# Two more output blocks of the last batch as Strassen products, their last stores in parts, and two of the first z turns copied by another engine

## The chip, the cores and the metric

The kernel runs on one core of a Trainium2 chip. The metric is the device time of one execution in microseconds (us); four executions are given for the kernel before. A core has a matrix engine, TensorE (PE in the profile, with its weight loads as PEld); a vector engine, VectorE (DVE); a scalar engine, ScalarE (ACT); GpSimd (POOL); and SyncE (SP), which here only issues DMAs. ACT and POOL issue DMAs too. Each engine runs its own instructions in order, and they wait for one another by semaphores. Matmuls write PSUM, which DVE and ACT read; everything else lies in the on-chip memory SBUF.

## The reference

Attention with squared positive scores, gated by `u`, then a feed-forward layer with a sigmoid gate. B is 8, S is 3008, D is 256, z has 64 columns, the hidden layer 2048.

```python
scores = scale * np.matmul(z, z.transpose(0, 2, 1))   # scale = 1 / S
attn = np.maximum(scores, 0.0) ** 2
x = (u * np.matmul(attn, v)).reshape(B * S, D)
h = x @ w_in
g = h * (1.0 / (1.0 + np.exp(-1.702 * h)))
out = g @ w_out
```

The scores are symmetric, since both sides are z.

## The kernel before

**Batches and blocks.** The eight batches follow one another. Within a batch the 3008 rows are cut into six column blocks of 512 (the last has 448; half a tile of 64 rows at the end of a batch is put together with that of its neighbour, so that an odd batch has a full last block and an even one a block of 384). Per batch the kernel runs attention for blocks 0 to 5, then the feed-forward layer for blocks 0 to 5. The order of every engine's instructions is that of the program text; nothing is reordered afterwards. PE's order is thus written out by hand: score matmuls (`take`, `scores`) are put between the steps of `attend` by the tables `SCHED`, `SCHED0`, `TAIL`, and so on.

**Attention.** `scores` multiplies z with z into a PSUM tile `sc`, two 512-wide halves at a time (from the tag `ps2`, two buffers). `square` lets ACT take the positive part (`rl`, L231) and DVE square it (`a`, L245). Where the mirrored block is wanted, SP issues a DMA that turns `a` into `tt` (L251). `attend` multiplies V with `a` or `tt` into `o` (L304), and DVE multiplies it with the turned `u` (L321).

**The start.** All engines are idle at first, and z of the first batch has to be turned before any scores can be made. Z comes in six pieces g of four tiles. `first_cast(g)` lets DVE write z in 16 bit twice side by side (L123); `first_zt(g)` lets PE transpose the four tiles into a PSUM tile `zp` (L129) and copies that to `ZT` with a rearrangement (L137): turn 0 by ACT, all others by DVE. Turns 0 and 1 stand before the loop. Turns 2 to 5 are put at steps n = 2, 7, 13 and 21 of the first `attend` (the table `FIRST_ZT`), and each is followed by the casts for the next turn. The pair of scores that needs turn 2 stands at step 6, that for turn 3 at step 14, that for turn 4 at step 22 (`SCHED0`). Meanwhile POOL casts V to 16 bit (L172), and SP issues the loads of z, V and the first u, and between them the turning DMAs.

**The feed-forward layer.** `up_group(b, q)` makes two of sixteen rows of hidden tiles for one block (four matmuls of 128x512, L345), ACT applies the gate (`gf`, L353) and DVE scales it to 16 bit (`gt`, L354). Eight groups make a block, 48 a batch; the first 20 are put between the steps of the last `attend`, and 28 are left.

The product with `w_out` is done in two ways. For blocks 0 to 3 (`k < NST`) it is one level of Strassen's scheme in Winograd's form: the block's row tiles are split by parity `o`, the hidden rows into halves and the output channels into halves `C0` and `C1`, and seven products P1 to P7 of half size take the place of eight. Each product (`product`, L441) is 16 matmuls of 128x128, each with its own weights. The left operands are sums S1 to S4 of parts of `gt`, made by DVE in two halves each (`left_sum`, L408 to L416); `up_group` takes one such sum from the list `SUMS` after its own work, so that they spread out. The products of a block share three PSUM tiles from the tag `ps1` (four buffers): P1, P6, P7 and P4 add onto one, P5 and P3 onto another, P2 has its own. After P1, P6 and P7 ACT copies the bank to a small SBUF tile (`uP1`, `uP6`, `uP7`, one buffer each, L451), before the next product adds on. The outputs are then: P2 + `uP1` (parity 0, `C0`), P5 + `uP7` after P7 (parity 1, `C1`), P5 with P3 + `uP6` after P3 (parity 0, `C1`), all by DVE (L457), and after P4 a copy by ACT (parity 1, `C0`, L453). `products` gives the order: each P1 of a block comes before P4 and P3 of the block before. After each of the 28 up groups stands one product, and 28 is also their number. After P3 of a block SP stores it.

Blocks 4 and 5 are done plainly. In batches 0 to 6 `down64` does it in 64-row pieces (L520), with the next batch's first scores in between. In the last batch `down` does it (L475): 16 matmuls of 128x256 per row tile, eight row tiles, with copies by ACT (L481) after every second one. `store` writes block 4 in one DMA, and the last block in three pieces of 128x2x256, 128x256 and twice 64x256, all issued by ACT (L493, L499).

**The queues around the change.** At the end SP's queue holds the stores of blocks 0 to 3, ACT's the copies and the stores of blocks 4 and 5, and POOL's nothing. At the start SP's queue holds the loads of z and V, then two turning DMAs, four loads of u (L187), and the rest of the turning DMAs.

Of the kernel before, what the change touches and what calls it, by code (L numbers as in the profile page):

```python
# [9 lines left out]
F32 = mybir.dt.float32  # L10
F16 = mybir.dt.float16
P = 128
# [3 lines left out]
def kernel(  # L16
# [13 lines left out]
    AF = mybir.ActivationFunctionType  # L30
# [9 lines left out]
    CH = 512  # L40
# [84 lines left out]
    def first_zt(g):  # L125
        z2 = ZT["st"][g // CB][:, g % CB * CB:(g % CB + 1) * CB]
        zp = ps1.tile([P, CB, P], F16, name="zp", tag="ps1")
        for k in range(CB):
            pe.transpose(zp[:, k, :], z2[:, k, :, :], ident)  # L129
        zt = ZT[0][:, g * CB:(g + 1) * CB, :].rearrange("d n p -> d (n p)")  # L130
        nb = CB if g < NCH - 1 else CB - 1
        dst = zt[:, :nb * P].rearrange("d (p n) -> d p n", n=nb)
        src = zp[:, :nb, :].rearrange("d n p -> d p n")
        if g == 0:
            act.activation(dst, src, AF.Copy, scale=1.0)
        else:
            dve.tensor_copy(dst, src)  # L137
        if nb < CB:
            dve.tensor_copy(zt[:, nb * P:], zp[:, nb, :])
# [194 lines left out]
    def blocks(b):  # L334

        return [(i, CH if i < NCH - 1 or b % 2 else LFULL) for i in range(NCH)]

    def up_group(b, q):
        k, fg = divmod(q, NFG)
        i, n = blocks(b)[k]  # L340
        hg = ps2.tile([P, FFG, CH], F32, name="hg", tag="ps2")
        for e in range(FFG):
            ff = fg * FFG + e
            for c in range(NCC):
                pe.matmul(  # L345
                    hg[:, e, :n], W1[:, c, ff * P:(ff + 1) * P], XT[b, i][:, c, :n],
                    start=(c == 0), stop=(c == NCC - 1),
                )
        if fg % 2 == 0:
            GT[b, k, fg // 2] = pa.tile([P, CB, CH], F16, name="gt", tag="tt", bufs=14)  # L350
        g = GT[b, k, fg // 2][:, (fg % 2) * FFG:(fg % 2 + 1) * FFG, :n]
        gf = pw.tile([P, FFG, CH], F32, name="gf", tag="gf")
        act.activation(gf[:, :, :n], hg[:, :, :n], AF.Gelu_apprx_sigmoid, scale=1.0 / FSC)  # L353
        dve.tensor_scalar(g, gf[:, :, :n], FSC, None, ALU.mult)  # L354
        if SUMS:
            SUMS.pop(0)()
        if k < NST and fg == NFG - 1:
            SUMS.extend(left_sums(b, k) + (weight_sums() if b == k == 0 else []))


# [3 lines left out]


    NST = 4
    SUMS, ST = [], {}
    LO, HI = slice(0, NFF // 2), slice(NFF // 2, NFF)
    C0, C1 = slice(0, P), slice(P, D)
# [45 lines left out]
        else:  # L415
            dve.tensor_tensor(s_, a12, ST[b, k, "S2", h], ALU.subtract)  # L416

    def products():

        lst = []  # L420
        for k in range(NST):
            one = [(k, "P6"), (k, "P5"), (k, "P7"), (k, "P2")]
            lst += [(k, "P1")] + ([(k - 1, "P4"), (k - 1, "P3")] if k else []) + one
        return lst + [(NST - 1, "P4"), (NST - 1, "P3")]

    def product(b, k, name):
        right = {
            "P1": W2[:, LO, C0], "P2": W2[:, HI, C0], "P3": W2[:, HI, C1], "P4": WT[:, 3],
            "P5": WT[:, 0], "P6": WT[:, 1], "P7": WT[:, 2],
        }[name]  # L430
        if name in ("P1", "P2", "P5"):
            ST[b, k, "bank" + name] = ps1.tile([P, 2, P], F32, name="st", tag="ps1")
        bank = ST[b, k, "bank" + {"P6": "P1", "P7": "P1", "P4": "P1", "P3": "P5"}.get(name, name)]
        for m in range(2):
            for ff in range(NFF // 2):
                h, f = divmod(ff, CB)
# [4 lines left out]
                pe.matmul(  # L441
                    bank[:, m, :], lhs()[:, f, m, :], right[:, ff, :],
                    start=name in ("P1", "P2", "P5") and m == 0 and ff == 0,
                    stop=ff == NFF // 2 - 1, skip_group_check=True,
                )
# [14 lines left out]
        if name == "P3":  # L460
            store(b, k, CB - 1, sp)

    def down_list(b):
        return [(k, s, h) for k, (i, n) in enumerate(blocks(b)) if k >= NST for s in range(n // P) for h in range(2)]

    def down(b, k, s, h):
        i, n = blocks(b)[k]
        ns = n // P
        if s == 0 and h == 0:
            Y[b, k] = pw.tile([P, CB, D], F32, name="y", tag="y")  # L470
        if s % 2 == 0 and h == 0:
            Y["ps"] = ps1.tile([P, 2, D], F32, name="yp", tag="ps1")
        yp = Y["ps"]
        for ff in range(h * NFF // 2, (h + 1) * NFF // 2):
            pe.matmul(  # L475
                yp[:, s % 2, :], GT[b, k, ff // CB][:, ff % CB, s * P:(s + 1) * P], W2[:, ff, :],
                start=(ff == 0), stop=(ff == NFF - 1),
            )
        if h == 1 and (s % 2 == 1 or s == ns - 1):
            s0 = s - s % 2  # L480
            act.activation(Y[b, k][:, s0:s + 1, :], yp[:, :s % 2 + 1, :], AF.Copy, scale=1.0 / FSC)  # L481
        if h == 1:
            store(b, k, s)

    def store(b, k, s, eng=act):
        i, n = blocks(b)[k]
        ns = n // P
        r0 = b * S + i * CH
        full = min(n, S - i * CH) // P
        final = b == B - 1 and k == NCH - 1  # L490
        if s == ns - 1 or final and s % 2 == 1:
            s0 = s - 1 if final else 0
            eng.dma_start(  # L493
                out[r0 + s0 * P:r0 + min(full, s + 1) * P].rearrange("(n p) c -> p n c", p=P),
                Y[b, k][:, s0:min(full, s + 1), :],
            )
        if s == ns - 1 and full < ns:
            for h_, bb in enumerate((b, b - 1)):
                (act if b == B - 1 else pool).dma_start(  # L499
                    out[bb * S + S0:(bb + 1) * S], Y[b, k][h_ * SREM:(h_ + 1) * SREM, full, :],  # L500
                )


    def down64(b, k):
# [8 lines left out]
        def step(n):  # L513
# [18 lines left out]
                        Y[b, k] = pw.tile([P, CB, D], F32, name="y", tag="y")  # L532
                    act.activation(Y[b, k][:, m * per:(m + 1) * per, :], yp[m][:, :per, :], AF.Copy, scale=1.0 / FSC)
            if n == len(order) - 1:
                store(b, k, ns - 1, pool)

        return turns, [lambda n=n: step(n) for n in range(len(order))]

# [51 lines left out]
    def take(b, n):  # L590
        for post_ in scores(b, [queue.pop(0) for _ in range(n)]):
            post_()
# [17 lines left out]
    posts[0]()  # L610
    first_cast(2)
    posts[1]()
    take(0, 1)
    load_u(0, 1)

    for b in range(B):
# [3 lines left out]
        for i in range(NCH):  # L620
            for n, step in enumerate(attend(b, i, b == 0 and i < 2)):
                if b == 0 and i == 0 and n == 5:
                    load_u(0, 0)
                if b == 0 and i == 0 and n in FIRST_ZT:
                    first_zt(FIRST_ZT[n])
                    if FIRST_ZT[n] + 1 < NCH:
                        first_cast(FIRST_ZT[n] + 1)
                if (i, n) in turn:
                    turn_u(b, turn[i, n])
# [10 lines left out]
        if more:  # L640
# [3 lines left out]
            for n0 in range(0, NJ, VB):  # L644
                load_v(b + 1, n0, sp)
            fill(b + 1)
        downs, prods = down_list(b), products()
        for q in range(head, nup):
            if more and q in (head + 14, head + 20):
                k = int(q == head + 20)  # L650
                turn_u(b + 1, k)
                load_u(b + 1, k + 2)
            up_group(b, q)
            product(b, *prods.pop(0))
        if more:
            while downs[0][0] < NCH - 2:
                down(b, *downs.pop(0))
            for k in range(NCH - 2, NCH):
                turns, steps = down64(b, k)
                at = {n: 3 - len(turns) for n in turns} | TAIL[len(turns)]  # L660
                for n, step in enumerate(steps):
                    take(b + 1, at.get(n, 0))
                    step()
        else:
            for d in downs:
                down(b, *d)


# [28 lines left out]
```

## Time and profile before

| what | us |
|---|---|
| four executions | 1207.62, 1209.11, 1210.41, 1211.33 |
| their median | 1209.76 |
| the profiled execution, by the same clock | 1211.33 |
| its span, first to last instruction | 1209.5 |

The profiled execution is one of the four. The granted TensorE clock was 0.999 over the span. The busy time of the engines by stretch, from the windows view:

```profile
0.00:10.00 10.00, 7.42 (x35) 2.68 (x35) 4.66 (x11) 5.49 (x6) 2.77 (x10) 1.00 0.76 240
10.00:20.00 10.00, 5.62 (x37) 2.30 (x36) 8.00 (x15) 4.14 (x5) 9.23 (x13) 1.00 1.15 264
20.00:30.00 10.00, 10.00 (x52) 3.33 (x50) 8.27 (x13) 7.69 (x8) 2.66 (x5) 1.00 1.22 175
...
1160.00:1170.00 10.00, 10.00 (x119) 7.45 (x118) 8.28 (x16) 7.13 (x10) 0.00 (x0) 1.00 0.01 3
...
1180.00:1190.00 10.00, 10.00 (x114) 7.17 (x112) 5.16 (x9) 6.43 (x9) 0.00 (x0) 1.00 0.17 54
1190.00:1200.00 10.00, 10.00 (x102) 9.04 (x100) 1.03 (x2) 2.22 (x3) 0.00 (x0) 1.00 0.22 73
1200.00:1210.00 10.00, 4.83 (x45) 4.08 (x42) 0.00 (x0) 1.19 (x2) 0.00 (x0) 1.00 0.27 86
```

Each row is a stretch from A to B in us after the start and its length, then the busy time and the number of instructions of PE, PEld, DVE, ACT and POOL, then the granted clock of PE, the mean busy share of the 16 DMA engines, and what they moved in GB/s. Between 10 and 20 us PE is busy 5.62 of 10 us; from 20 us on it is busy throughout, until after 1200 the matmuls end. In the rows quoted below, "x16" counts instructions of one kind that follow each other, and a time in brackets is idle time of that engine and who ended it.

### The profile page before, as it was taken

Reading aid. Unit: us, or ns where it says so; the run is one execution under the profiler, and the core shown is the slowest. Engines: PE = TensorE matmul, PEld = TensorE weight load, DVE = VectorE, ACT = ScalarE, POOL = GpSimd, SP = SyncE. Lnnn points to the kernel's source line nnn. Section 1 sums busy time; section 2 is a strip of 40 time slices with the busy share of each in tenths; the row PEclk is TensorE's granted clock in tenths of the full one; section 3 lists DMA queues with packets and bytes.
Section 4 is the critical chain, followed back from the end, with each engine's and each line's share of the span. In section 5 each row is a group of like instructions: output and inputs, shape, how many; then the busy total and the mean of one; then the engine's idle time right before and its main releaser. Section 6 shows DMA issues by size and latency. Waiting matters only on the chain.

```text
span 1209.5 us, 28025 instructions
## 1 busy us (share of the span) xinstructions
PE 1193.3 (99%) x11689; PEld 718.7 (59%) x11689; DVE 819.0 (68%) x1257; ACT 768.6 (64%) x897; POOL 306.4 (25%) x361
## 2 busy tenths in 40 slices
PE   7999999999999999999999999999999999999998
PEld 2446765467654685446765468554775547844576
DVE  6669954597546975469654696648966489564882
ACT  5777684476845767357683666736677376762763
POOL 4145300452004620044200451015510134101000
PEclk9999999999999999999999999999999999999999
DMA  9966389562994539854399443974449764596012
GB/s 228 164 110 126 117 167 156 89 150 74 182 158 85 140 93 173 147 85 136 93 188 140 81 137 97 192 131 77 139 122 188 126 88 146 115 175 112 1 37 70
DMA packets 366111, 152.32 MB, mean 126 GB/s; under 512 B 313248, under 2 KB 358048, under 8 KB 365984
## 3 DMA queue, kind: packets, MB, share of 16 engines
q1 hardware_dynamic: 328960, 113.16, 48.1%
q0 software_dynamic: 35392, 35.80, 14.6%
q8 instruction: 91, 1.49, 0.5%
q10 hardware_dynamic: 1632, 1.57, 0.4%
q14 instruction: 36, 0.29, 0.1%
HBM read 60.29 MB, written 24.64 MB: 70 GB/s over the span
## 4 chain that ended last, share of the span: by engine, by line
PE 96%; DMA 2%; DVE 1%; ACT 1%; issue 0%; SPq 0%; ACTq 0%
PE o L304 38%; PE hg L345 26%; PE st L441 17%; PE yp L520 8%; PE sc L217 6%; DMA tt<-a 1%; PE yp L475 1%; DVE a L245 1%; ACT rl L231 0%; DMA zf<-in_z_dram 0%; DVE gt L354 0%; DVE zst L123 0%; ACT gf L353 0%; DVE ZT L137 0%; DVE s L414 0%
## 5 line engine op out<-in xcount | busy, mean ns | idle before, releaser
L353 ACT ACTIVATE gf<-hg 128x1024 f32<-128x1024 f32 (+1 forms) x384 | 385.8, 1007 | 165.6 <-PE hg L345 137.9
L231 ACT ACTIVATE rl<-sc 128x1024 f16<-128x1024 f32 x311 | 308.1, 1025 | 213.7 <-PE sc L217 211.6
L304 PEld LDWEIGHTS <-V 64*128 64x128 f16 (+1 forms) x4052 | 237.0, 95 | 251.5 <-issue 12.7
L345 PE MATMUL hg<-xt,W 128*128 128x512 f16 (+1 forms) x1408 | 354.5, 374 | 0.1
L354 DVE TENSOR_SCALAR gt<-gf 128x1024 f16<-128x1024 f32 (+1 forms) x384 | 275.6, 718 | 92.8 <-ACT gf L353 89.3
L245 DVE TENSOR_TENSOR a<-rl 128x1024 f16<-128x1024 f16 x276 | 191.8, 696 | 187.4 <-ACT rl L231 184.5
L304 PE MATMUL o<-a,V 64*128 64x512 f16 (+2 forms) x2010 | 317.6, 373 | 0.0
L187 POOL DMA_DIRECT2D uq<-in_u_dram x188 | 129.5, 696 | 516.3 <-PE sc L217 347.2
L304 PE MATMUL o<-tt,V 64*128 64x512 f16 (+1 forms) x1762 | 215.6, 376 | 4.3 <-DMA tt<-a 4.3
L345 PEld LDWEIGHTS <-W 128*128 128x128 f16 x1536 | 141.2, 98 | 117.4 <-issue 0.3
L441 PEld LDWEIGHTS <-gt 128*128 128x128 f16 x2048 | 125.1, 98 | 28.5
L217 PE MATMUL sc<-ZT 64*128 64x512 f16 (+1 forms) x692 | 121.9, 367 | 3.1 <-DVE ZT L137 2.7
L441 PEld LDWEIGHTS <-s 128*128 128x128 f16 x1536 | 93.8, 98 | 21.0
L172 POOL CAST V<-vst 128x512 f16<-128x512 f32 x96 | 90.1, 975 | 63.2 <-DMA vst<-in_v_dram 50.2
L520 PE MATMUL yp<-W,gt 64*128 64x256 f16 x1664 | 104.0, 269 | 0.0
L520 PEld LDWEIGHTS <-gt 64*128 64x128 f16 x1664 | 80.6, 94 | 19.1 <-POOLq L84 4.1
L321 DVE TENSOR_TENSOR xt<-o,ut 128x512 f16<-128x512 f32 x80 | 51.4, 685 | 39.3 <-PE o L304 39.3
L441 PE MATMUL st<-WT,s 128*128 128x128 f16 x1024 | 67.6, 219 | 0.0
L441 PE MATMUL st<-WT,gt 128*128 128x128 f16 x1024 | 67.6, 219 | 0.0
L441 PE MATMUL st<-W,gt 128*128 128x128 f16 x1024 | 67.6, 219 | 0.0
L217 PEld LDWEIGHTS <-ZT 64*128 64x128 f16 x692 | 37.9, 94 | 39.0 <-issue 7.2
L194 DVE STREAM_TRANSPOSE ut<-uq 128x1024 f32<-128x1024 f32 (+1 forms) x48 | 58.3, 1215 | 0.0
(49 smaller groups left out, 618.3 us busy)
## 6 DMA issues: line engine op xcount, KB each, us to landing
vst<-in_v_dram SPq DMA_DIRECT2D x39, 512.0 KB, 4.8
uq<-in_u_dram POOLq DMA_DIRECT2D x156, 128.0 KB, 3.5
out_dram<-y SPq DMA_DIRECT2D x32, 512.0 KB, 3.7
tt<-a SPq DMA_TRANSPOSE x230, 3.4
uq<-in_u_dram POOLq DMA_DIRECT2D x32, 112.0 KB, 2.9
out_dram<-y POOLq DMA_DIRECT2D x7, 512.0 KB, 4.9
vst<-in_v_dram SPq DMA_DIRECT2D x8, 384.0 KB, 4.6
out_dram<-y POOLq DMA_DIRECT2D x7, 384.0 KB, 4.5
```

The source lines that it names most:

```text
L172: pool.tensor_copy(V16[b][:, n0:n0 + VB, k, :].rearrange("p n (q c) -> p n q c", c=QW), vst.rearrange("p n (q k c) -> p n q k c", k=NCC, c ...
L187: eng.dma_start(uq[k * QW:(k + 1) * QW, :n // QW].rearrange("t q k c -> t q (k c)"), src[:, :, cs])
L194: dve.transpose(ut[:, :, :n // QW, :].rearrange("p k q t -> p q k t"), UQ.pop((b, i))[:, :n // QW])
L217: pe.matmul(sc[:, r, :m * P], zt[h, 2 * kp + r, :], zt[h, (qi + 1) * CB - m:(qi + 1) * CB, :], start=True, stop=True,)
L231: act.activation(rl, sc, AF.Relu, scale=csc)
L245: dve.tensor_tensor(a, rl, rl, ALU.mult)
L304: ins = pe.matmul(acc[c][:, :n], V16[b][h, j, c, :], weights(b, i, j)[h], start=(k, m) == first[c], stop=(k, m) == final[c],)
L345: pe.matmul(hg[:, e, :n], W1[:, c, ff * P:(ff + 1) * P], XT[b, i][:, c, :n], start=(c == 0), stop=(c == NCC - 1),)
L353: act.activation(gf[:, :, :n], hg[:, :, :n], AF.Gelu_apprx_sigmoid, scale=1.0 / FSC)
L354: dve.tensor_scalar(g, gf[:, :, :n], FSC, None, ALU.mult)
L441: pe.matmul(bank[:, m, :], lhs()[:, f, m, :], right[:, ff, :], start=name in ("P1", "P2", "P5") and m == 0 and ff == 0, stop=ff == NFF // ...
L520: ins = pe.matmul(yp[s // per][:, s % per, :], GT[b, k, ff // CB][h, ff % CB, s * P:(s + 1) * P], W2[h, ff, :], start=new, stop=n == last[ ...
```

## The change

It has two parts that don't touch each other.

At the start: z turns 2 and 3 are copied by ACT, as turn 0 is, and the casts for turn 3 stand before the third pair's scores (`take(0, 1)`) instead of after turn 2. The casts for turns 4 and 5 keep their places.

In the last batch: `nst(b)` is six instead of four, so blocks 4 and 5 become Strassen products too, with their S sums. `products` then gives 42 products; the 28 up groups take the first 28, up to (4, P1) and (3, P4), and the other 14 follow one after another, the first four of them preceded by two sums each, which are block 5's eight. The function `down` and its plain matmuls are gone. Block 4 is stored by SP after its P3. Block 5 is stored in four parts as they become ready, by `store_part`: after P7 and P4 the odd row tiles of one channel half (one DMA of 128x128 by SP, one of 64x128 by ACT and one by POOL), after P2 and P3 the even ones (one DMA of 128x2x128 by SP). In batches 0 to 6 the instructions are the same as before.

```diff
-        if g == 0:
+        if g in (0, 2, 3):
             act.activation(dst, src, AF.Copy, scale=1.0)
         else:
             dve.tensor_copy(dst, src)
...
-        if k < NST and fg == NFG - 1:
+        if k < nst(b) and fg == NFG - 1:
             SUMS.extend(left_sums(b, k) + (weight_sums() if b == k == 0 else []))
...
+    def nst(b):
+        return NST if b < B - 1 else NCH
...
-        if name == "P3":
-            store(b, k, CB - 1, sp)
...
+        if b == B - 1 and k == NCH - 1:
+            if name in ("P2", "P7", "P4", "P3"):
+                store_part(b, k, *{"P4": (1, C0)}.get(name) or outs[name][:2])
+        elif name == "P3":
+            store(b, k, sp)
+
+    def store_part(b, k, o, c):
+
+        r0 = b * S + k * CH
+        y = Y[b, k].rearrange("p (m o) c -> p m o c", o=2)[:, :, o, c]
+        if o == 0:
+            dst = out[r0:r0 + 3 * P].rearrange("(s t) c -> t s c", t=P)[:, ::2, c]
+            sp.dma_start(dst, y)
+            return
+        sp.dma_start(out[r0 + P:r0 + 2 * P, c], y[:, 0])
+        for h in range(2):
+            r1 = (b - h) * S + S0
+            (act, pool)[h].dma_start(out[r1:r1 + SREM, c], y[h * SREM:(h + 1) * SREM, 1])
...
+    first_cast(3)
     take(0, 1)
...
-                    if FIRST_ZT[n] + 1 < NCH:
+                    if 3 <= FIRST_ZT[n] < NCH - 1:
                         first_cast(FIRST_ZT[n] + 1)
...
-        downs, prods = down_list(b), products()
+        prods = products(nst(b))
...
             up_group(b, q)
             product(b, *prods.pop(0))
+        for kp in prods:
+            for s_ in SUMS[:2]:
+                s_()
+            del SUMS[:2]
+            product(b, *kp)
...
-        else:
-            for d in downs:
-                down(b, *d)
```

More of the change, by code (lines that the diff above doesn't have):

```diff
@@ L416, in left_sum, with products @@
             dve.tensor_tensor(s_, a12, ST[b, k, "S2", h], ALU.subtract)
-    def products():
+    def products(n):
         lst = []
-        for k in range(NST):
+        for k in range(n):
             one = [(k, "P6"), (k, "P5"), (k, "P7"), (k, "P2")]
             lst += [(k, "P1")] + ([(k - 1, "P4"), (k - 1, "P3")] if k else []) + one
-        return lst + [(NST - 1, "P4"), (NST - 1, "P3")]
+        return lst + [(n - 1, "P4"), (n - 1, "P3")]
     def product(b, k, name):
@@ L459, in product @@
             )
-        if name == "P3":
-            store(b, k, CB - 1, sp)
-    def down_list(b):
-        return [(k, s, h) for k, (i, n) in enumerate(blocks(b)) if k >= NST for s in range(n // P) for h in range(2)]
-    def down(b, k, s, h):
-        i, n = blocks(b)[k]
[L468 to L483, printed above, removed]
@@ L485, in store @@
-    def store(b, k, s, eng=act):
-        i, n = blocks(b)[k]
-        ns = n // P
+        if b == B - 1 and k == NCH - 1:
[14 more added lines that the diff above has]
+            (act, pool)[h].dma_start(out[r1:r1 + SREM, c], y[h * SREM:(h + 1) * SREM, 1])
@@ L488, in store @@
+    def store(b, k, eng):
+        i, n = blocks(b)[k]
         r0 = b * S + i * CH
         full = min(n, S - i * CH) // P
[L490 to L497, printed above, removed]
+        eng.dma_start(out[r0:r0 + full * P].rearrange("(n p) c -> p n c", p=P), Y[b, k][:, :full, :])
+        if full < n // P:
@@ L498, in store @@
             for h_, bb in enumerate((b, b - 1)):
-                (act if b == B - 1 else pool).dma_start(
+                pool.dma_start(
                     out[bb * S + S0:(bb + 1) * S], Y[b, k][h_ * SREM:(h_ + 1) * SREM, full, :],
@@ L534, in step @@
             if n == len(order) - 1:
-                store(b, k, ns - 1, pool)
+                store(b, k, pool)
         return turns, [lambda n=n: step(n) for n in range(len(order))]
@@ L654 @@
             product(b, *prods.pop(0))
+        for kp in prods:
[3 more added lines that the diff above has]
+            product(b, *kp)
         if more:
-            while downs[0][0] < NCH - 2:
-                down(b, *downs.pop(0))
-            for k in range(NCH - 2, NCH):
+            for k in range(NST, NCH):
                 turns, steps = down64(b, k)
```

## The prediction

> **What bounds the kernel now.** I read the busy times first, then the chain that ended last, then what TensorE (PE) waited for, then both ends of the timeline.
>
> ```profile
> PE 1193.3 (99%) x11689; PEld 718.7 (59%) x11689; DVE 819.0 (68%) x1257; ACT 768.6 (64%) x897; POOL 306.4 (25%) x361
> PE 96%; DMA 2%; DVE 1%; ACT 1%; issue 0%; SPq 0%; ACTq 0%
> PE o L304 <- DMA tt<-a: 4.3, 4, 2.2
> PE zp L129 <- DVE zst L123: 2.9, 2, 2.4
> PE sc L217 <- DVE ZT L137: 2.7, 2, 2.0
> ```
>
> PE is the bound; off the chain nothing counts. Its waits (total us, times, longest) are few: four on turned attention blocks, all after 480 us, and four in the first 18 us, on DVE. A PE microsecond saved at either end should reach the end, if no wait replaces it.
>
> The first microseconds (start, us, engine, line, tile; in brackets the idle time and who ended it):
>
> ```profile
> 8.33 1.94 ACT L231 ACTIVATE rl<-sc 128x1024 f16<-128x1024 f32 x2 [0.35 <-PE sc L217]
> ...
> 8.76 2.71 DVE L245 TENSOR_TENSOR a<-rl 128x1024 f16<-128x1024 f16 x3
> ...
> 11.39 0.68 DVE L137 COPY ZT<-zp 128x512 f16<-128x512 f16 x1
> ...
> 12.13 0.61 PE L217 MATMUL sc<-ZT 64*128 64x512 f16 x4 [1.96 <-DVE ZT L137]
> ...
> 15.46 0.68 DVE L137 COPY ZT<-zp 128x512 f16<-128x512 f16 x1
> ...
> 16.06 0.90 DVE L123 CAST zst<-zf 128x256 f16<-128x256 f32 x2
> 17.01 0.40 PE L129 MATMUL zp<-ident,zst 128*128 128x128 f16 x4 [2.42 <-DVE zst L123]
> ```
>
> The 11.39 copy is z turn 2; its transposes ended at 9.31 (row "8.92 0.39 PE L129"), but three squares stand before it on DVE. ACT is free from 10.27. The 15.46 copy is turn 3; behind it the casts of turn 4 are late, and PE stands 2.42. That makes 4.38 us of idle PE. From 17.01 on PE has no idle time until the first of the four waits on tt, at 482.
>
> The last microseconds:
>
> ```profile
> 1189.80 1.06 PE L441 MATMUL st<-W,s 128*128 128x128 f16 x16
> ...
> 1190.70 14.14 PE L475 MATMUL yp<-W,gt 128*128 128x256 f16 x128
> ...
> 1204.87 0.60 ACT L481 ACTIVATE y<-yp 128x512 f32<-128x512 f32 x1 [2.90 <-PE yp L475]
> 1205.50 0.35 ACTq L493 DMA_DIRECT2D out_dram<-y  x1
> 1205.89 1.19 ACTq L499 DMA_DIRECT2D out_dram<-y  x2
> ```
>
> After the last matmul (1204.84): copy 0.60, three stores issued one behind another on ACT; the last issue starts near 1206.5, lands 2.0 later (64 KB rows of the issue table), and 0.95 remains to 1209.5. Together 4.65.
>
> **The change, part by part.**
>
> *z turn 2 on ACT.* It follows the pair of rl that ends at 10.27, overlapping by 0.1 as that pair does (two of 1.02 in 1.94), and takes 0.60 (turn 0: "4.96 0.60 ACT L135"): done 10.78. PE started 0.05 after turn 0's copy, so its scores start at 10.83, not 12.13: 1.30 less. The Trainium skill, page "ScalarE: Activation LUTs", section "Rules for kernel authors", advises VectorE for simple elementwise work, up to three times faster per element in 16 bit. Here the same 128x512 f16 copy took 0.60 on ACT and 0.68 to 0.69 on DVE; by the rule's factor ACT would take 3 x 0.68 = 2.0, end at 12.2, and nothing would be gained here. The row decides. The copies need no other ACT table: turn 0 is the same Copy.
>
> *Casts of turn 3 ahead of the third and fourth squares, turn 3 to ACT.* The moved casts are two (0.5 to 0.9 a pair) and delay those squares, and the two transposes that SP issues from them (10.48), by that much. PE has other steps until then. SP's four loads of u follow (issued 15.59 to 17.76); DVE turns that u at 25.54, or near 23.4 then; landing moves from about 21.7 to 22.7. It fits by 0.7; if it fails, DVE waits, and behind it squares that PE needs only for the next query block. Between the fifth and sixth squares and turn 4's casts, the 15.46 copy (0.60 of pitch) goes. So the 17.01 wait ends 1.30 + 0.60 = 1.90 earlier. Bounds: 1.6 if the delayed squares push the fifth one by 0.3; 2.5 if DVE, then beside fewer POOL casts, runs the sixth square in 0.69 instead of 1.01 (near POOL casts squares stretch to 1.07). Taken: **2.1**. Behind it PE has work at every step and the next turn's copies have half a microsecond of slack. The transposed blocks that SP moves for batch 0 keep over 3 us before use, and batch 0 had no wait there, so this carries to the end.
>
> *16 more half-block sums (S1 to S4) on DVE.* Block 4's eight lie in block 5's up groups, one per 1.76 us round. DVE was busy 5.16 of 10 us there, against 8.2 in the same rounds with sums at 1150 to 1170, where PE has no gap: no cost. Block 5's eight stand in the tail, below.
>
> *Tail matmuls.* Six blocks of seven products are 42; 28 up groups carry 28 of them, as now, and 14 stand bare at the end: (3,P3), then block 4's and 5's from (4,P6). So 128 matmuls of 128x256 in 13.98 (109.2 ns each) become 14 products of 16 of 128x128. One such product is 0.894 (chain of waits: "0.89 PE st L441 x16"; 55.9 ns each): 12.52. PE saves **1.46**, if it holds that pace. The rule against it: "TensorE: Matmul & The Clock Gate", section "Back-to-back issue gap", gives about 81 ns per matmul for a sustained stream of weight load and N=128 matmul pairs. By it: 224 x 81 = 18.1, a loss of 4.2 in this part. Our trace has only runs of 16 at this width, but within them each of the 15 gaps is 56 ns, and PEld shows each load starting with the matmul before it, no earlier: there is no stock of finished loads that a longer run would use up. For instruction supply, the 64-row pairs of L520 (at 300 to 316 us) hold four PE instructions per 109 ns, 27 ns each, for twenty steps; the tail needs 28. I take 55.9.
>
> *Waits that the tail adds.* Products were spaced by up groups; now they touch. DVE runs in order: last gt 1191.06, S4 of block 4, two S1 of block 5, then the output sum after (3,P3), six more S, then the output sums of block 4. From start to start a sum takes 0.605 (gt 1155.93, sum 1156.54, output 1157.14), an output, 0.42 long, about 0.34. Output (3,P3) runs 1193.48 to 1193.90. The uP6 buffer is single, so ACT's copy after (4,P6), whose product ended at 1192.65, waits for it: 1193.95 to 1194.33. (4,P7) adds onto the same bank, could start at 1193.38 and starts at 1194.38: **stall 1.0**. Queued behind that ACT copy are only later tail copies. Next: (4,P3) needs the output sum after (4,P7), which stands behind the S sums until 1197.86; PE reaches it at 1197.96, just after. Later copies (uP1, uP6, uP7 of block 5) come 0.2 us or more ahead. Stall bounds: 0 (if DVE runs tighter) to 1.9 (if (4,P3) waits another 0.9, a product's length). PE ends at 1190.70 + 12.52 + 1.0 + 0.16 = 1204.38, 0.46 earlier.
>
> *Last stores.* They go out after P7, P2, P4 and P3, on SP, ACT and POOL; only the last, 128 KB on SP, follows the last product: output 0.03 + 0.42, handover 0.03, landing 1.7 to 2.1 after issue as the 128 and 256 KB rows of ACT's stores, then 0.95: 3.4 instead of 4.65, **1.25** less. The part on POOL after P4 is issued near 1204.0. Nearest rows: 64 KB on POOL 4.4 (behind other stores, DMA busy), u loads on POOL 2.5 at best. With 2.5 it lands before SP's; with 4.4 near 1208.4, 1.5 later, eating the whole gain. DMA share is 0.27 here, so I take 2.7.
>
> **Sum.** 2.1 + 0.46 + 1.25 = 3.8. The profiled execution took 1211.33 (span 1209.5 plus 1.8 around), the slowest of four: 1207.5 there. The median of those shown is 1209.76: **1206.0**. The 4.3 us of waits on turned blocks, part of what scatters those runs, are in both kernels.
>
> **Rivals.** A measurement of this kernel tells 0.2% (2.4 us) from no change.
> - *Forecast, both ends gain*: 1206.0. Chance 0.62.
> - *Only the head gains*: stall 1.9 instead of 1.0, and the POOL store lands 1.5 after SP's: the tail gives 1.7 - 0.9 - 0.9 (the stall postpones both stores alike, some of POOL's delay overlaps) = about 0: 1207.7. For: DVE is late by 1.7 us in the tail and POOL's rows are long. Against: idle DMA. 0.18.
> - *Only the tail gains*: moved casts, POOL's casts and SP's late transposes hold PE elsewhere in the first 30 us: 1209.76 - 1.7 = 1208.1. Against: 7 free steps and ACT's idle time. 0.10.
> - *Slower: weight loads set the tail's pace.* At p ns a matmul the tail takes 0.224p instead of 13.98, stall gone, head and stores still giving 3.35: it decides from (13.98 + 3.35) / 0.224 = 77 ns. At the rule's 81 ns 1210.6; at 98 ns, which one recorded load lasts, 1214.4. For: rule and length. Against: the 56 ns gaps. 0.10.
>
> That the change doesn't do what it says is no rival: the instruction order shows the 224 products, two copies on ACT, and nothing else moved.
>
> **Range and chances.** Own bounds: head 1.6 to 2.5; tail 0.2 (stall 1.9, POOL late) to 2.7 (no stall): 1204.6 to 1208.0; with a median's scatter of near 1 us 1203.6 to 1209.0, which takes in the two middle rivals. Faster: 0.6 of the forecast and some 0.1 of the middle rivals, 0.70; same 0.22; slower 0.08.
>
> **What would show it.** Head: ACT copies at 10.2 and 13.1; waits on ZT under 0.8 us at 10.8, on zst ending near 15; scores of turn 3's columns near 15.6, not 17.56. Tail: 16-matmul products 0.89 apart; one wait of 1.0 of PE st on ACT, none over 0.3 after; last product's end near its stores by 3.4. Wrong if gaps in the tail exceed 70 ns, if (4,P3) waits too, or if PE waits on tt in batch 0.

## The result and the profile after

| | before | changed |
|---|---|---|
| median, us | 1209.99 (59 runs, 1206.24 to 1215.39) | 1207.36 (38 runs, 1204.05 to 1210.76) |
| ratio | | 0.9976, interval 0.9969 to 0.9983 |
| the profiled execution, us | 1211.33 | 1205.77 |
| its span, us | 1209.5 | 1204.0 |

By the ratio the change makes the kernel faster by 2.9 us (2.1 to 3.75); the medians differ by 2.6. The profiled executions differ by more, 5.5 us of span; where that lies is told below.

Line numbers of the Strassen part are higher by four after the change: the product is L445 (was L441), the copy to `uP` L455 (L451), ACT's output L457 (L453), DVE's output L461 (L457). First the list of what PE waited for, in us in total, times, and the longest:

```profile
PE zp L129 <- DVE zst L123: 2.7, 2, 2.4
PE o L304 <- DMA tt<-a: 1.7, 4, 0.5
...
PE st L445 <- ACT uP L455: 0.9, 1, 0.9
PE sc L217 <- DVE ZT L137: 0.8, 1, 0.8
PE sc L217 <- ACT ZT L135: 0.6, 1, 0.6
```

The two waits on ZT, 2.7 us before, are 0.8 and 0.6. One wait on `uP` is new. The wait on zst, 2.4 us before, is still 2.4. The waits on turned blocks are 1.7 instead of 4.3; none of them is in the first batch, and the change doesn't touch what they wait for.

The timeline of the head (PE, DVE and ACT, rows of other work left out):

```profile
10.00 0.60 ACT L135 ACTIVATE ZT<-zp 128x512 f16<-128x512 f16 x1
...
10.66 0.60 PE L217 MATMUL sc<-ZT 64*128 64x512 f16 x4 [0.64 <-ACT ZT L135]
...
12.91 0.60 ACT L135 ACTIVATE ZT<-zp 128x512 f16<-128x512 f16 x1
14.09 1.31 DVE L123 CAST zst<-zf 128x256 f16<-128x256 f32 x2
...
15.46 0.40 PE L129 MATMUL zp<-ident,zst 128*128 128x128 f16 x4 [2.35 <-DVE zst L123]
...
16.07 1.03 PE L217 MATMUL sc<-ZT 64*128 64x512 f16 x4
...
17.03 2.78 PE L304 MATMUL o<-a,V 128*128 128x512 f16 x7
...
20.18 0.60 PE L217 MATMUL sc<-ZT 64*128 64x512 f16 x4
```

ACT makes both copies where it was meant to. The scores of turn 2 start at 10.66 (12.13 before), the transposes of turn 4 at 15.46 (17.01), the scores of turn 3 at 16.07 (17.56). So PE is 1.5 us ahead at 16. Then it loses it: the four scores at 16.07 take 1.03 instead of 0.60, the seven matmuls of L304 2.78 instead of 1.68, and the scores that wait for turn 4's columns (the last row) start at 20.18, as against 20.15 before. The windows view says what happened (the columns as in the windows shown before):

```profile
12.46:15.87 3.41, 1.06 (x8) 0.38 (x6) 2.94 (x4) 1.06 (x2) 3.41 (x6) 1.00 1.19 283
15.87:19.28 3.41, 3.41 (x11) 1.01 (x11) 2.72 (x5) 1.94 (x2) 3.41 (x6) 0.50 1.33 222
```

PE's granted clock is 1.00 up to 15.87 and 0.50 for the next 3.41 us. In the profile of before there is such a drop too, of 3.41 us from 482.97 on, behind the 2.19 us wait on a turned block:

```profile
479.56:482.97 3.41, 1.22 (x12) 0.38 (x10) 1.10 (x2) 0.98 (x1) 0.00 (x0) 1.00 0.92 137
482.97:486.38 3.41, 3.41 (x19) 1.19 (x17) 1.04 (x2) 1.94 (x2) 0.00 (x0) 0.50 1.04 195
```

PE was busy throughout it, so it cost time there, and after has no drop at that place.

The tail:

```profile
1189.38 0.42 DVE L461 SCALAR_TENSOR_TENSOR y<-st,uP 128x256 f32<-128x256 f32 x1
...
1189.89 0.38 ACT L455 ACTIVATE uP<-st 128x256 f32<-128x256 f32 x1 [2.68 <-DVE y L461]
1190.33 1.05 PE L445 MATMUL st<-WT,gt 128*128 128x128 f16 x16 [0.94 <-ACT uP L455]
...
1191.22 1.95 PE L445 MATMUL st<-W,gt 128*128 128x128 f16 x32
...
1200.80 0.37 SPq L476 DMA_DIRECT2D out_dram<-y  x1
```

The chain of the one stall can be read upward: DVE's output of (3,P3) ends at 1189.80, ACT's copy after (4,P6) waits for that output because there is one `uP6` buffer, and (4,P7), whose wait is in the third row, stands 0.94 for the copy. The products behind it are 0.89 apart. From the end of the last up group to the end of the span it is 18.17 us, 19.57 before: 1.40 less. Of these, 0.37 are PE's (from the last up group to the last matmul 14.50 instead of 14.87), and 1.03 lie behind the last matmul (3.67 instead of 4.70).

So the 5.5 us between the two spans are, to within 0.2: 2.6 of waits on turned blocks (0.8 to 9.7 us in all, in the profiles of this case), 1.7 of the clock drop behind one of them (half of 3.41), 1.4 of the tail, and nothing of the head, since this execution gave it back.

### The profile page after: what moved, and what is told of

The parts are those of the page before. It is cut to its first block, busy times and chain, and to the rows that moved or that the text cites. A ratio compares the mean times of both kernels' runs of the same rounds, so it can differ in the third digit from the quotient of the medians.

```text
span 1204.0 us, 28259 instructions
## 1 busy us (share of the span) xinstructions
PE 1191.9 (99%) x11785; PEld 716.6 (60%) x11785; DVE 830.3 (69%) x1277; ACT 770.3 (64%) x903; POOL 308.9 (26%) x363
## 4 chain that ended last, share of the span: by engine, by line
PE 95%; DMA 2%; DVE 2%; ACT 1%; issue 0%; SPq 0%; ACTq 0%; DVEq 0%
PE o L304 37%; PE hg L345 26%; PE st L445 17%; PE yp L511 8%; PE sc L217 6%; DMA tt<-a 2%; DVE a L245 1%; ACT rl L231 0%; DVE gt L354 0%; DMA zf<-in_z_dram 0%; DVE zst L123 0%; ACT gf L353 0%; DVE s L416 0%; DVE s L418 0%; PE zp L129 0%
## 5 line engine op out<-in xcount | busy, mean ns | idle before, releaser
L304 PEld LDWEIGHTS <-V 64*128 64x128 f16 (+1 forms) x4052 | 235.1, 94 | 250.8 <-issue 11.6
L304 PE MATMUL o<-a,V 64*128 64x512 f16 (+2 forms) x2010 | 317.6, 372 | 0.0
L304 PE MATMUL o<-tt,V 64*128 64x512 f16 (+1 forms) x1762 | 215.4, 376 | 1.8 <-DMA tt<-a 1.7
L445 PEld LDWEIGHTS <-gt 128*128 128x128 f16 x2176 | 132.4, 98 | 29.8 <-issue 1.1
L445 PEld LDWEIGHTS <-s 128*128 128x128 f16 x1632 | 99.2, 98 | 20.7
L445 PE MATMUL st<-WT,gt 128*128 128x128 f16 x1088 | 71.8, 219 | 0.9 <-ACT uP L455 0.9
L445 PE MATMUL st<-W,gt 128*128 128x128 f16 x1088 | 71.7, 219 | 0.0
L445 PE MATMUL st<-WT,s 128*128 128x128 f16 x1088 | 71.5, 219 | 0.0
L455 ACT ACTIVATE uP<-st 128x256 f32<-128x256 f32 x102 | 39.1, 383 | 40.4 <-DVE y L461 35.1
```

The source lines that it names most:

```text
L304: ins = pe.matmul(acc[c][:, :n], V16[b][h, j, c, :], weights(b, i, j)[h], start=(k, m) == first[c], stop=(k, m) == final[c],)
L445: pe.matmul(bank[:, m, :], lhs()[:, f, m, :], right[:, ff, :], start=name in ("P1", "P2", "P5") and m == 0 and ff == 0, stop=ff == NFF // ...
```

## The experiments

Twelve kernels were run, one of them the changed kernel again. Each edit is given against the changed kernel unless it says otherwise; ratios are to the kernel before, timed beside it; they are not the ratios of the medians, and where the two differ both are given. "Turn 4's scores" means the start of the first scores that need turn 4's columns, 20.15 before and 20.18 after; "the tail" is the time from the end of the last up group to the end of the span, 19.57 before and 18.17 after.

| kernel | median, us | ratio and interval | turn 4's scores | tail |
|---|---|---|---|---|
| head alone | 1208.26 | 0.9990 (0.9981 to 0.9998) | 20.29 | 19.57 |
| tail alone | 1207.78 | 0.9983 (0.9974 to 0.9992) | 20.28 | 18.15 |
| product ahead of its two sums | 1206.00 | 0.9965 (0.9951 to 0.9978) | 20.37 | 18.00 |
| eight matmuls in the stand | 1205.46 | 0.9961 (0.9948 to 0.9973) | 18.71 | 18.18 |
| one sum behind each product | 1205.31 | 0.9964 (0.9952 to 0.9976) | 19.44 | 17.06 |
| last block stored whole | 1207.44 | 0.9981 (0.9970 to 0.9992) | 18.76 | 18.94 |
| turn 4's casts early | 1203.78 | 0.9959 (0.9943 to 0.9974) | 17.30 | 18.17 |
| both mended, turn 4 on ACT | 1203.40 | 0.9956 (0.9938 to 0.9974) | 16.84 | 17.08 |
| changed kernel again | 1207.02 | 0.9978 (0.9965 to 0.9990) | 20.36 | 18.17 |
| early casts and one sum each | 1204.44 | 0.9952 (0.9933 to 0.9971) | 17.93 | 17.07 |
| eight matmuls and one sum each | 1204.07 | 0.9951 (0.9932 to 0.9970) | 18.70 | 17.07 |

**The two parts alone.** The head alone is the kernel before with the three pieces of the change's diff that lie in the first batch; its last batch keeps four Strassen blocks, `down` and the stores of before.

For the tail alone the head is as it was:

```diff
-        if g in (0, 2, 3):
+        if g == 0:
...
-    first_cast(3)
     take(0, 1)
...
-                    if 3 <= FIRST_ZT[n] < NCH - 1:
+                    if FIRST_ZT[n] + 1 < NCH:
```

> Only the first batch is changed (turns 2 and 3 on ACT, casts of turn 3 early); the tail is that of before. Theory A (both parts gain, the clock drop seen in the changed kernel's profile from 15.9 to 19.3 us is chance): the fourth turn's transposes start near 15.5 instead of 17.0, and the median is 1.2 to 1.6 us below before. Theory B (the longer work without PE before 15.5 makes the clock drop in nearly every run, and the drop takes the gain back): PE reaches the scores of turn 4's columns near 20.2 as before, clock 0.5 for 3.4 us before that, median within 0.4 us of before.

> Only the last batch is changed (42 Strassen products, stores in parts); the head is that of before. Theory A: 1.2 to 1.7 us below before, with one wait of 0.94 of PE on an ACT copy, the first of 14 bare products to the span's end 17.4 against 18.8. Theory B: the whole measured gain of 2.9 is here.

By the ratios the head alone is faster than before by 1.2 us (0.2 to 2.3) and the tail alone by 2.1 (1.0 to 3.1); the medians differ by 2.0 and 2.5 from the 1210.26 of 28 runs of before. The sum of the two, 3.3, is more than the change gives, but the intervals are 2.1 us wide each, so the totals don't show an interaction. For the head the total fits theory A better, and the profile theory B. Its tail is 19.57, as before, and its transposes of turn 4 start at 15.56; then the clock falls at 15.86 and turn 4's scores start at 20.29:

```profile
15.56 0.40 PE L129 MATMUL zp<-ident,zst 128*128 128x128 f16 x4 [2.35 <-DVE zst L123]
...
17.25 2.67 PE L304 MATMUL o<-a,V 128*128 128x512 f16 x7
...
20.29 0.61 PE L217 MATMUL sc<-ZT 64*128 64x512 f16 x4
```

How a head that is given back in its profile can be worth 1.2 us in the runs is taken up at the end of the next section. The tail alone has the stall of 0.94 and 1.4 us less of tail, so that part does its work without the head. It had a clock drop as well, from 13.92 on, with the old order of the head:

```profile
12.00:15.40 3.40, 2.82 (x14) 1.14 (x15) 2.82 (x5) 1.94 (x2) 3.21 (x6) 0.78 1.23 299
15.40:17.00 1.60, 0.93 (x4) 0.03 (x2) 1.53 (x4) 0.00 (x0) 1.43 (x3) 0.50 1.15 255
```

There it cost almost nothing (turn 4's scores at 20.28 instead of 20.15): PE ran slowly where it would have stood for zst, and its waits on zst are 0.9 us in all, not 2.9. In the new head the drop came behind the stand and found none to hide in.

**The clock.** Dummy matmuls of zeros ahead of turn 4's transposes keep PE busy while it stands, and change nothing else; the casts of turn 4 at step 6 take the stand itself away.

```diff
                 if b == 0 and i == 0 and n in FIRST_ZT:
+                    if FIRST_ZT[n] == 4:
+                        warm_up(8)
                     first_zt(FIRST_ZT[n])
```

```diff
-                    if 3 <= FIRST_ZT[n] < NCH - 1:
+                    if 4 <= FIRST_ZT[n] < NCH - 1:
                         first_cast(FIRST_ZT[n] + 1)
...
+                if b == 0 and i == 0 and n == 6:
+                    first_cast(4)
                 take(b, sched[i].get(n, 0))
```

> The changed kernel with eight dummy 128x512 matmuls of zeros (no result uses them) before the transposes of turn 4, where PE stands 2.35 us. Theory A (the clock drops by chance, in some runs): clock 1.0 from 6 to 30 us, transposes of turn 4 still near 15.5, turn 4's scores near 18.6; median 0.3 to 1.0 below the changed kernel. Theory B (it drops in nearly all runs): the same profile, median 1.5 to 1.8 below the changed kernel. If the clock isn't governed by idle PE: still 0.5 somewhere, no gain.

> The changed kernel, but the casts of turn 4 stand before the fifth and sixth squares on DVE instead of after them. Theory A (a long stretch without PE before turn 4's transposes makes the clock drop, and DVE's order makes the stretch): transposes of turn 4 near 13.5, no wait of PE over 1.2 us after 9 us, clock 1.0 from 6 to 30 us, scores of turn 4 near 17.6 instead of 20.2; median 1.5 to 2.6 below the changed kernel. Rival (the clock drops by itself in the first 20 us, the wait has no part in it): a stretch at 0.5 stays and the scores come after 18.8.

With the dummies PE's head reads:

```profile
15.57 0.40 PE L129 MATMUL zp<-ident,zst 128*128 128x128 f16 x4 [0.64 <-DVE zst L123]
...
16.12 0.61 PE L217 MATMUL sc<-ZT 64*128 64x512 f16 x4
16.65 1.68 PE L304 MATMUL o<-a,V 128*128 128x512 f16 x7
...
18.71 0.61 PE L217 MATMUL sc<-ZT 64*128 64x512 f16 x4
```

The transposes start no earlier than in the changed kernel (15.57 against 15.46), yet turn 4's scores start 1.47 earlier: the matmuls run at 0.61 and 1.68 again. The total is 1.6 to 1.9 below the changed kernel's by the medians and 1.8 to 2.1 by the ratios. Early casts do more in the head:

```profile
12.94 0.40 PE L129 MATMUL zp<-ident,zst 128*128 128x128 f16 x4
...
16.75 0.40 PE L129 MATMUL zp<-ident,zst 128*128 128x128 f16 x4 [1.04 <-DVE zst L123]
...
17.30 0.60 PE L217 MATMUL sc<-ZT 64*128 64x512 f16 x4
```

The transposes of turn 4 start at 12.94, PE's longest stand in the head behind the first scores, 1.04, is now before turn 5, and turn 4's scores start at 17.30, 2.9 earlier. The median is 3.2 to 3.6 lower, but the ratio only 2.1 to 2.3 us, since one of the eight runs took 1209.63; so the totals don't show that early casts do more than the dummies.

One profile each could be chance. Each run also reports its mean granted clock, and a mean of 1.0 means that no whole drop of 3.41 us fell on it (one takes 0.0014 off). Of the runs with the head as in the change (the changed kernel twice, the head alone, and the three kernels that differ only in the tail) 12 of 91 have 1.0; of those with dummies or early casts (the two above, and each with the mended tail) 18 of 26. The runs of before timed beside them have it in 7 of 73, so drops are no rarer in the kernel before; what the new head changes is where a drop falls and what it costs. Among the changed kernel's 39 runs, the profiled one with them, the seven at 1.0 have a median of 1205.5, the others of 1207.7.

**The tail's stall.** In the first edit the product is issued before its two sums:

```diff
         for kp in prods:
+            product(b, *kp)
             for s_ in SUMS[:2]:
                 s_()
             del SUMS[:2]
-            product(b, *kp)
```

In the second, one sum follows each product:

```diff
         for kp in prods:
-            for s_ in SUMS[:2]:
-                s_()
-            del SUMS[:2]
             product(b, *kp)
+            if SUMS:
+                SUMS.pop(0)()
```

> The changed kernel, but in the bare tail each product and its outputs come before the two sums that now stand before it, so that DVE does the output after (3,P3) ahead of block 5's first sums. Theory A (the 0.94 wait comes from DVE's order alone): the wait of PE on the ACT copy after (4,P6) falls below 0.1, no other appears, first bare product to the span's end 16.5 instead of 17.45, median 0.9 below the changed kernel. Rival (DVE's work in the tail is too much in any order): the wait moves to (4,P3) or to block 5's P6 and stays over 0.5 in sum, no gain.

> The changed kernel, but in the bare tail each product and its outputs come first, and one sum of block 5 follows each of the first eight products, not two each of the first four. Theory A (PE waited because outputs stood behind sums on DVE and every copy buffer uP is single; the work itself fits): no wait of PE over 0.1 us in the tail, last up group's end to the span's end 17.2 instead of 18.17 in the changed kernel, the whole 0.94. Rival (DVE has too much work in any order): a wait of 0.5 or more stays somewhere, as the 0.77 before block 5's P6 did with outputs first.

The first did not do what it was for. The stall of (4,P7) is gone, but another takes its place:

```profile
1193.38 0.38 ACT L455 ACTIVATE uP<-st 128x256 f32<-128x256 f32 x1 [3.49 <-DVE y L461]
...
1193.81 1.95 PE L445 MATMUL st<-WT,s 128*128 128x128 f16 x32 [0.77 <-ACT uP L455]
```

The copy after block 5's P1 waits for DVE's output of block 4 that reads the one `uP1` buffer, and that output now stands behind the two S4 sums. The tail gains 0.17 only. The median is 1.0 to 1.4 below the changed kernel's, about the 0.9 expected of a tail without the stall, but the tail doesn't explain it; totals of some ten runs don't resolve this part, and the profiles decide. With one sum behind each product DVE's output comes earlier, and the copy after (4,P6) lets (4,P7) start at once:

```profile
1188.43 0.38 ACT L455 ACTIVATE uP<-st 128x256 f32<-128x256 f32 x1 [1.48 <-DVE y L461]
1188.96 1.06 PE L445 MATMUL st<-WT,gt 128*128 128x128 f16 x16
```

No wait of PE on `uP` is left, and the tail is 17.06, 1.11 less than the changed kernel's, which is the 0.94 of the stall and some 0.17 that stopping and starting cost besides. So the stall came from the order of DVE's queue, as the prediction had it, and another order removes it.

**The last stores.** Block 5 is stored after its P3 in one DMA of 384 KB by SP, and its two halves of a row tile, 64 KB each, by ACT.

```diff
-        if b == B - 1 and k == NCH - 1:
-            if name in ("P2", "P7", "P4", "P3"):
-                store_part(b, k, *{"P4": (1, C0)}.get(name) or outs[name][:2])
-        elif name == "P3":
-            store(b, k, sp)
+        if name == "P3":
+            store(b, k, sp, act if b == B - 1 else None)
```

> The changed kernel, but the last block is stored after P3 as a whole: 384 KB by SP, and two remainders of 64 KB one behind another by ACT. Theory A (the parts save what they take off the end): last matmul to the span's end 4.2 to 4.7 instead of 3.67, so that 0.5 to 1.0 of the tail's gain is the stores'. Rival (the end is a fixed price of landing and closing): 3.7 to 3.9.

From the last matmul to the end of the span it takes 4.43 instead of 3.67: the parts are worth 0.76. The median is the changed kernel's within the interval. The clock did not drop in this profile, though its head is the same and PE stands as long:

```profile
15.62 0.40 PE L129 MATMUL zp<-ident,zst 128*128 128x128 f16 x4 [2.35 <-DVE zst L123]
...
16.16 0.61 PE L217 MATMUL sc<-ZT 64*128 64x512 f16 x4
16.70 1.68 PE L304 MATMUL o<-a,V 128*128 128x512 f16 x7
```

Turn 4's scores start at 18.76. A stand of 2.35 us thus does not always bring the drop. Why it does so at times is taken up in the last section.

**Both mended.** Three kernels have the tail with one sum behind each product. Two of them have the early casts too, the first of these with turn 4 copied by ACT:

```diff
-        if g in (0, 2, 3):
+        if g in (0, 2, 3, 4):
```

In the third the dummies stand in for the early casts. The changed kernel, unedited, was run again beside the latter two, and came out as it was expected to.

> e5's tail and e7's head together, and turn 4 copied by ACT as well. Both theories A: the gains add, 2.5 to 3.8 us below the changed kernel, near 1204.3, 0.47% below before. If either falls: at most 2 below the changed kernel.

> The changed kernel itself, beside the mended ones on one chip. 2.0 to 3.3 us below before, as measured. In its profile: turn 4's transposes at 15.4 to 15.7 (or near 16.3 if the clock drops before 12 us), turn 4's scores at 18.7 without a clock drop after 15 us and near 20.2 with one; the tail 18.17 from the last up group to the span's end.

> The tail of one sum after each product, and the casts of turn 4 ahead of the fifth and sixth squares; turn 4 stays on DVE. Theory (the long waits on turned blocks in batch 0, which some runs with both mended had, come from running 1.3 us or more further ahead of SP's turning DMAs): most runs near 1203, and here too a run or more in ten 4 us or more above the median. Rival (they came from turn 4's copy on ACT alone): no such run. Median 3 to 4 below the changed kernel either way.

> The tail of one sum after each product, and eight dummy matmuls of zeros before turn 4's transposes, DVE's order as in the changed kernel. It runs 1.5 us behind the version with earlier casts in batch 0, so by the same theory it has fewer or no runs 4 us above the median; clock 1.0 from 13 to 30 us; median 1.5 to 2.5 below the changed kernel, near 1205.

All three are faster than before, by 5.3 to 5.9 us by the ratios. Their ratios lie 0.0020 to 0.0027 below the changed kernel's, 2.4 to 3.3 us, with intervals that overlap at the edge. Which of them is best can't be told, and the early casts show no lead over the dummies in the total. Whether the two gains add up isn't settled either: from early casts alone to early casts with the tail mended, worth 1.1 in the profile, the ratio falls by 0.0007, 0.8 us, while the median rises from 1203.78 to 1204.44.

The first of the three has the lowest runs (1200.14), and 4 of 12 at 1207 to 1212. Its profile caught one of these, with the list of waits

```profile
PE o L304 <- DMA tt<-a: 9.7, 5, 5.8
...
PE zp L129 <- DVE zst L123: 0.9, 2, 0.5
```

and this window:

```profile
40.00:50.00 10.00, 4.24 (x22) 1.52 (x22) 2.22 (x4) 2.10 (x4) 0.00 (x0) 0.66 1.25 174
```

PE stands 5.76 us up to 45.88 for a turned block of the first batch. SP issued two of the turning DMAs in 6.75 and 6.25 us (at 23.10 and 31.30), where those of before take 1.2 to 2.8 in this stretch and those of the other profiles at most 4.7, and everything behind them in SP's queue was late. The DMA engines were about as busy in the same window of before (a share of 1.21, here 1.25), so that alone doesn't explain it. With turn 4's scores at 16.84, PE asks for the turned blocks earlier than in any other profile here. The two theories of the last expectations don't come out clean, though: long runs came with early casts and turn 4 on DVE (one of eight at 1209.63, one of six at 1207.67), against the rival that ACT's copy makes them, and with the dummies too, which leave PE further behind (one of seven at 1208.69), against the theory that the lead makes them. Runs of before reach 1215.16 and 1216.28. What makes the two issues long stays open.

**V's casts beside DVE's.** To see whether POOL's casts of V lengthen DVE's casts for turn 4, POOL writes only one half of the channels of V for tiles 4 to 23 of the first batch; the attention of that batch reads this half twice, so a part of V is left out.

```diff
-        for k in range(NCC):
+        for k in range(NCC if b or n0 < VB else 1):
...
-                    acc[c][:, :n], V16[b][h, j, c, :], weights(b, i, j)[h],
+                    acc[c][:, :n], V16[b][h, j, c if b or j < VB else 0, :], weights(b, i, j)[h],
```

> The changed kernel, in which POOL makes only the first channel half of V's 16-bit copy for tiles 4 to 23 of the first batch, and the first batch's attention reads that half twice (part of V is left out). Theory (turn 4's transposes come at 15.46 and not at the forecast 14.9 because DVE's squares and casts take 1.0 to 1.1 and 0.70 beside POOL's casts, 0.69 and 0.28 alone): with half the POOL casts DVE's row of squares and casts from 9.2 to 15.4 shortens by 0.5 to 1.5 us, transposes at 14.0 to 15.0. Rival (the length is set by ACT and the order of waits): 15.3 or later.

The transposes of turn 4 start at 15.46, so by the number that was written down the rival is right. That number can't decide, though: in this profile the clock was 0.5 from 7.76 to 11.17, so that turn 2's scores started at 11.56, 0.90 later than in the changed kernel, and DVE had to wait for them. What can be compared is the stretch behind it, on DVE:

```profile
13.05 0.69 DVE L245 TENSOR_TENSOR a<-rl 128x1024 f16<-128x1024 f16 x1 [1.67 <-ACT rl L231]
13.97 1.03 DVE L245 TENSOR_TENSOR a<-rl 128x1024 f16<-128x1024 f16 x1 [0.23 <-ACT rl L231]
14.92 0.48 DVE L123 CAST zst<-zf 128x256 f16<-128x256 f32 x2
```

The two casts take 0.48, where they took 1.31 in the changed kernel, and no cast of V ran beside them. The square before them still took 1.03, with a cast of V beside it. From the scores of turn 2 to the transposes of turn 4 it is 3.90 us, 4.80 in the changed kernel. So the casts of V do lengthen DVE's casts, by 0.83; that a full clock would then have put the transposes near 14.6 is worked out, not shown.

## Why the prediction was right, and where its sizes were off

It forecast 3.8 us and the runs show 2.9, inside the range. The total alone doesn't tell the forecast (1206.0) from its middle rivals (1207.7 and 1208.1): 2.9 below 1209.76 is 1206.9, between them. The tail was forecast rightly in its mechanism. The head's gain was made as forecast, but in most profiles it did not reach the end, so that the total still fits is in part luck. By its own steps:

- **Turn 2 on ACT, 1.30.** Right: 1.47 measured, of which 0.14 is an earlier landing of z. ACT's copy took 0.60, as turn 0's had; the threefold rule weighed against it does not hold for this copy.
- **The head's 2.1.** Mis-sized twice. First, the transposes of turn 4 start 1.55 earlier, not 2.1 or the 1.90 of the sum without the credit. The term that failed is the pair of turn 4's casts: taken over as they were in the trace of before (0.90), they took 1.31, since POOL's casts of V ran beside both; and the fifth and sixth squares took 1.01 and 1.09 (0.91 and 1.01 before), not the 0.69 that the credit had hoped for. 1.90 less 0.41 is 1.49, about what was measured. Second, "behind it PE has work at every step, so this carries to the end" is the step that failed. It has work, but in four of six profiles with this head (the changed kernel twice, the head alone, the product ahead of its sums) half the clock for 3.41 us falls on that work, which costs 1.5 us, as the dummies show, and takes the whole gain back. The granted clock of 0.999 over the span stood ahead of the prediction, which never asked what a stand of 2.4 us does to it. In a profile without the drop there, the whole store's, the head is worth 1.4 at turn 4's scores (18.76 instead of 20.15).
- **The casts of turn 3 and u.** No harm, as forecast: SP issued the loads of u at 14.96 (15.59 before). The two moved casts took 1.32, more than the 0.5 to 0.9 allowed for, but the fifth square still started at 12.14, right behind its `rl` (12.11).
- **Pace of the tail, 55.9 ns.** Right. The row of 32 matmuls in 1.95 us and those next to it keep 0.89 a product, through 224 matmuls in all; behind the stall each starts 56 ns after the one before it. The rule that had been weighed against it, 81 ns per pair of weight load and matmul, and with it the slower rival, is refuted for these runs.
- **The stall, 1.0.** Right in place and cause, 0.94; (4,P3) came just in time, as reckoned. The gain on PE was 0.37, forecast 0.46. One sum behind each product gives it back.
- **The last stores, 1.25.** 1.03 measured, of which the parts are 0.76. The last DMA landed 1.82 after its issue, within the bounds. What was mis-sized is the end behind it, taken as 0.95 and measured as 1.36. SP ends the program by waiting for the semaphores of the DMAs one after another, 0.06 us apart; before the change the last landing was the last but one on that list, in the changed kernel seven more waits follow it. POOL's part landed 1.92 after its issue (2.7 taken), so the rival with the late POOL store had no ground.

Added up by what was measured, 1.4 + 0.37 + 1.03 = 2.8 without a drop of the clock behind the stand and 1.4 with one that isn't hidden. The measured 2.9 is at the upper end of that, and the head alone is worth 1.2 in its runs, although most profiles with this head have the drop. What can make up for it is that the kernel before loses to drops as well: 13 of its 73 runs have a mean clock of 0.997 or less, of those with the new head 1 of 91. In before's one profile the drop lies at 482.97, in that of the tail alone it is hidden in the stand. Where it falls in the other runs is not recorded, so the split of the total between the parts stays open by about a microsecond.

## What to carry to other kernels

A stand of the matrix engine can cost more than its length: when it is moved or shortened, look at what the clock does right behind it, and read the gain at a later point than the one where the edit acts. In an in-order queue, sums that are needed later belong behind the outputs that free a buffer now, but in small portions; two at a time moved the stall, one at a time removed it. Before a duration is carried to another place, see what ran beside it: the same two casts took 0.48, 0.90 and 1.31 us here.

## What the runs showed of the hardware

**The clock is set from windows on a fixed grid.** In one profile the clock fell at 16.19 and again at 1204.03, behind the end of the matmuls; that is 348.0 times 3.413 us. If the stretches of 3.413 us are laid back from a drop in each of the fourteen profiles, and the matmuls of the trace summed in each stretch, then, between the first 3 us and the last matmuls, all eight stretches with PE busy for 0.39 or less of the time were followed by half the clock, two of seven with 0.48 to 0.52 were, and none with 0.55 or more. The grid's place differs between runs: behind the same stand the drop came at 15.86, 15.87, 16.19 and 16.76. In the changed kernel the grid put the stand into one stretch (1.06 of 3.41, shown above). In the kernel with the whole store the same stand was cut by a border of the grid:

```profile
11.17:14.59 3.42, 2.10 (x15) 0.82 (x11) 3.41 (x5) 2.43 (x3) 3.42 (x4) 1.00 1.14 348
14.59:18.00 3.41, 2.38 (x15) 1.00 (x16) 2.78 (x6) 1.40 (x2) 3.41 (x7) 1.00 1.14 225
```

Neither stretch is less than 0.6 busy, and the clock stays at 1.00 behind them too. So the same stand costs 1.5 us more in some runs than in others, by where the grid cuts it. The Trainium skill, "TensorE: Matmul & The Clock Gate", section "Part 1: The HAM clock gate", states a window of 3413 ns that runs freely, which these traces confirm; it lets the clock fall after an idle window, which is not needed here: a window with a third of matmuls in it is enough.

**Two engines side by side.** The pair of casts on DVE took 0.48 us with nothing on POOL and 1.31 with POOL's casts of V beside both, 2.7 times as long.
